# One GpSimd shift for two pattern groups, and two changes to the zero products, in a two-attention kernel

## The chip, the core and the metric

The kernel runs on one core of one Trainium2 chip. The metric is the device time of one launch in microseconds (us), and a smaller time is better. A core has a matrix engine (TensorE; PE in the profile, with its weight loads listed apart as PEld), a vector engine (VectorE, DVE), a scalar engine (ScalarE, ACT), GpSimd (POOL), and an engine that here only issues transfers (SyncE, SP). Each works through its own list of instructions in order and waits at semaphores for the others.

## The reference, cut to what matters

Two independent attention blocks A and B work on inputs of 2048 rows by 512 columns in bfloat16, with 32 heads of width 16; their outputs are joined side by side.

```python
# A: linear attention
phi = lambda t: jnp.where(t > 0, t + 1, jnp.exp(t)) + 1e-6
pq, pk = phi(q), phi(k)
kv  = jnp.einsum("bhsd,bhse->bhde", pk, v)
num = jnp.einsum("bhqd,bhde->bhqe", pq, kv)
den = jnp.einsum("bhqd,bhd->bhq", pq, jnp.einsum("bhsd->bhd", pk))[..., None] + 1e-6
a = merge_heads(num / den) @ wo
# B: softmax attention
scores = jnp.einsum("bhqd,bhkd->bhqk", q, k) * 16 ** -0.5
p = softmax(scores)
b = merge_heads(jnp.einsum("bhqk,bhkd->bhqd", p, v)) @ wo
out = jnp.concatenate([a, b], axis=-1)
```

B's scores are 32 heads of 2048 by 2048 numbers, each of which needs an exponential. That is nearly all of the work.

## The kernel before, in words

**Units and blocks.** B is cut into 32 units: four groups of eight heads, times four pieces of 512 queries, times two halves of the eight heads (`unit`). In a unit, four heads stand in four row strips of TensorE (`g` = 0 to 3), and the 2048 keys are cut into 16 pieces of 128, so a unit has 64 blocks of 128 keys by 512 queries. For each block `qk` (L807) makes the scores in PSUM, something takes the exponential, and a product with the values (L1142) adds the block to the unit's sum in `PVb` (pPV in the profile). A column of ones beside the values gives the softmax denominator.

**Two ways to an exponential.** Most blocks go the ACT way: two or three blocks lie side by side in one of two PSUM slots of `S5` (pS), and one ScalarE instruction (L1018) writes their exponentials to `PT`. The others go the D way: their scores go to a bank of `DB` (pD) or to a spare bank of pS, and VectorE (L923) turns them into 16-bit integers whose bits, read as float16, are a rough exponential. `DI` holds eight groups of up to two such blocks. To refine the result, two more patterns are made by adding a constant to the integers of the whole group (`shift`, for v = 1 and v = 2). GpSimd does this (L1071), or for v = 2 now and then VectorE (L1068). A block of the D way thus takes three products L1142 instead of one: with the values `VV` for the first two patterns and with scaled values `VX` for one.

**The rest.** In between lie "jobs": projections of q, k and v for later units, all of attention A (with exponentials `EA`, L630, on ScalarE), its output projections (L745) and some checks of the input's size. At a unit's end VectorE transposes pPV (L1171), takes reciprocals, and GpSimd normalizes (L1177).

**Who sets the order.** Nothing is chosen on the chip. While the kernel is built, a planner keeps an estimated clock `T` for each engine, holds candidates (`push`, `cands`, `pv_cand`, `job_cand`, `fill_act_cand`, `fill_d_cand`), and picks again and again the one that could start first. A priority breaks ties. It then writes the instruction into that engine's list. Estimated durations stand at each `push`, and the constants at the head of the function bound the choices: `PW` weighs groups not yet shifted in GpSimd's backlog, `JM` is the number of PSUM banks that jobs may hold, `DBL` and `PBL` bound the backlogs of VectorE and GpSimd at which blocks still take the D way, `FPB` and `FDB` bound when a third block may go to ScalarE, `PTA` tells when `PT` is scarce, `PSH` and `DSH` decide which engine shifts v = 2, and `PM` is when GpSimd's result counts as ready, measured from its estimated end. So a change of a constant or of one choice moves everything that follows.

**Zero products.** TensorE is kept busy in places by products with a tile of zeros: `warm` (L1255) issues 30 at the very start, and `fill_in` (L1399) puts some in when the planner sees TensorE waiting for its next step.

**Start and end.** The first two tiles of x come by a transposing load, the next two are transposed by TensorE (L1266), and then the first projections (L1277) lead to the first scores. After the last unit, VectorE works through its two halves (L1232 to L1237), and the last output projections of B (L1194) and four stores (L1247) follow.

Of the kernel before, what the change touches and what calls it, by code (L numbers as in the profile page):

```python
# [9 lines left out]
F16 = mybir.dt.float16  # L10
I16 = mybir.dt.int16
ACTF = mybir.ActivationFunctionType
ALU = mybir.AluOpType
# [225 lines left out]
def bass_concat_heads__linear_attn_block__softmax_full_mha__prompt_kernel(nc, A_x, A_wqkv, A_wo, B_x, B_wqkv, B_wo, out):  # L239
# [6 lines left out]
    NU = NGP * NC * 2  # L246
    SC = 0.25
    VST = 136
    LAY = (25, 8)
    PW = 0.7  # L250
    JM = 2
    JX = 1
    NB = 2
    NPT = LAY[0]
# [11 lines left out]
    ALAG = 100.0  # L266
    DLEAD = 0.8
    DPR = 3.0
    DBL = 2.0
    PBL = 7.0  # L270
    SEG = ()
    GB = 0.0
    PM = -0.05
    AEND = 60.0
    RW = 0.3
    EQ = 26.0
    FPB = 5.0
    FDB = 1.5
    FNR = 2
    AJP = 2.5  # L280
    HP = 0.5
# [1 line left out]
    BJ0 = 30.0  # L283
    D0 = 14.0
    RMX = 4
    XAL = 7.0
    NZ = 0
    SD = 0
    PTA = 4
    PTD = 1  # L290
    PSH = 2.5
    DSH = 1.0
    FM = 0.06
    JB = True
    WARM = (30,)
    TRACE = None


# [5 lines left out]
    with es:  # L304
# [629 lines left out]
                waiting[bi] = (buf, b, push("dve", en + LAT, 0, 0.6, p1))  # L934

        dgroup["st"] = {}

        def bank_at(at):

# [114 lines left out]
        def chain(buf):  # L1054
            s_ = dgroup["st"][buf]
            if not s_["closed"] or len(s_["items"]) < s_["taken"]:
                return
            s_["chained"] = True
            n = len(s_["items"])
            w = 512 * n  # L1060
            src = DI[:, buf, D0_:D0_ + w]
            rk = [("DI", 0, buf, i) for i in range(n)]

            def shift(v, t_):
                def r(st_, en_, lane="pool"):
                    if lane == "dve":
                        wide = w + 32
                        sch.add(lane, lambda e: e.tensor_scalar(gapped(DI[:, buf, :], DIV[v], wide // 32, 32), DI[:, buf, D0_ - 32:D0_ + w], 1.0, float(SHIFT[v - 1]),  # L1068
                                                                op0=ALU.mult, op1=ALU.add), reads=rk, writes=[("DI", v, buf)])
                    else:  # L1070
                        sch.add(lane, lambda e: e.tensor_scalar(DI[:, buf, DIV[v]:DIV[v] + w], src, 1.0, float(SHIFT[v - 1]), op0=ALU.mult, op1=ALU.add),  # L1071
                                reads=rk, writes=[("DI", v, buf)])
                    for i, b in enumerate(s_["items"]):
                        if lane == "dve":
                            P = gapped(DI.bitcast(F16)[:, buf, :], DIV[v] + 33 + i * 528, 16, 32)
                        else:
                            P = DI.bitcast(F16)[:, buf, DIV[v] + i * 512:DIV[v] + (i + 1) * 512]
                        pv_ready[b[0]].append((en_ + (PM if lane == "pool" else LPE["dve"]), b, (P, ("DI", v, buf)), ("d", buf), "VX"[v - 1]))
                if v == 2 and p_backlog(t_) - DSH * d_backlog(t_) > PSH:
                    push("dve", t_, 1, 0.06 + (w + 32) * 0.00053, lambda st_, en_: r(st_, en_, "dve"))  # L1080
                else:
                    push("pool", t_ + LAT + 0.05, 0, 0.276 + w * 0.00083, r)
            for v in (1, 2):
                shift(v, s_["t"])

# [80 lines left out]
        def unit_done(u, t_):  # L1166
# [96 lines left out]
        for t, bk, lane in ((2, SBANKS[1], "dve"), (3, SBANKS[2], "act")):  # L1263
            def tr(e, t=t, bk=bk):
                for cc in range(4):
                    ins = e.transpose(bfv(bk)[:, cc * 128:(cc + 1) * 128], ONL[:, t, cc * 128:(cc + 1) * 128], identb[:])  # L1266
# [143 lines left out]
        while True:  # L1410
# [157 lines left out]
```

## Time and profile before

| | |
|---|---|
| time of three runs | 673.05, 674.85, 674.97 us; median 674.85 |
| the profiled execution | 674.9 us, of which its span, first to last instruction, is 673.2 us |
| instructions in the span | 16020 |
| data read from and written to HBM | 4.46 MB and 4.19 MB |

The profile names a group of instructions by engine, by line of the kernel and by what it writes and reads (`out<-in`). In the table of groups, "x" is the number of instructions, then come the group's busy time in us and the mean duration of one in ns, and after the bar the engine's idle time just before them with what ended it. Instructions of one engine overlap: the next one begins while the one before it is still finishing. A mean duration is thus longer than the distance from one to the next. The chain of waits follows the last instruction backwards through whatever released each step, and its pieces do not overlap.

### The profile page before, as it was taken

To read this page: it belongs to the slowest core of one execution; us is meant where nothing else is said; L and a number is where in the kernel's file an instruction comes from. 1 tells how busy PE (TensorE), PEld (TensorE's weight loads), DVE (VectorE), ACT (ScalarE), POOL (GpSimd) and SP (SyncE) were. 2 spreads that over 40 slices of the span, in tenths; PEclk is the share of its full clock that TensorE was granted. 3 is DMA by queue.
4 is the path that set the end of the run, shared out by engine and by line. 5 is a ranking of instruction groups with operands and counts; after the bars stand their busy time and mean duration, and the time that the engine had idled before them with its cause. 6 is when DMAs were issued, how large, how long until landed. Compare 5 with 4: busy or idle time off the path is not lost.

```text
span 673.2 us, 16020 instructions
## 1 busy us (share of the span) xinstructions
PE 651.9 (97%) x6628; PEld 204.4 (30%) x6628; DVE 623.5 (93%) x1051; ACT 657.4 (98%) x691; POOL 589.7 (88%) x603
## 2 busy tenths in 40 slices
PE   8999999999999999999999999999999999999997
PEld 5323332223333333222222322322224222222222
DVE  3999999999989999999999999999999999999993
ACT  5999999999999999999999999999999999999995
POOL 5898898998989998989898999989899889898893
PEclk9999999999999999999999999999999999999999
DMA  9602001101011101110111110100000010001101
GB/s 215 161 2 33 1 9 34 40 10 38 4 33 32 32 2 33 34 47 10 40 40 18 32 25 25 17 9 10 9 25 2 17 33 33 1 33 41 32 33 37
DMA packets 53216, 21.56 MB, mean 32 GB/s; under 512 B 44176, under 2 KB 52624, under 8 KB 53136
## 3 DMA queue, kind: packets, MB, share of 16 engines
q1 hardware_dynamic: 51808, 19.94, 12.7%
q8 instruction: 54, 0.88, 0.5%
q10 hardware_dynamic: 1328, 0.52, 0.3%
q14 instruction: 26, 0.21, 0.1%
HBM read 4.46 MB, written 4.19 MB: 13 GB/s over the span
## 4 chain that ended last, share of the span: by engine, by line
ACT 93%; PE 5%; DVE 1%; DMA 1%; issue 0%; ACTq 0%
ACT PT L1018 90%; ACT EA L630 2%; PE pPV L1142 1%; PE pS L807 1%; DVE DI L923 1%; PE pD L745 1%; DMA xTb<-in_B_x_dram 1%; PE pS L1277 0%; PE pS L1399 0%; PE pS L1194 0%; DVE KNa L519 0%; PE pD L1277 0%; DVE OT L1171 0%; PE pD L1194 0%; ACTq L1512 0%
## 5 line engine op out<-in xcount | busy, mean ns | idle before, releaser
L1018 ACT ACTIVATE PT<-pS 128x1024 f16<-128x1024 f32 (+1 forms) x652 | 648.5, 1307 | 2.7 <-PE pS L807 2.3
L1071 POOL TENSOR_SCALAR DI<-DI 128x1024 int16<-128x1024 int16 x529 | 553.1, 1046 | 60.7 <-DVE DI L923 24.2
L923 DVE TENSOR_SCALAR DI<-pD 128x512 int16<-128x512 f32 (+1 forms) x453 | 315.0, 710 | 20.3 <-PE pD L807 12.4
L807 PE MATMUL pS<-QT,KM 32*128 32x512 bf16 x1570 | 256.8, 385 | 12.1 <-ACT PT L1018 7.7
L1142 PE MATMUL pPV<-PT,VV 128*17 128x512 f16 x1397 | 238.3, 381 | 0.3 <-ACT PT L1018 0.3
L1142 PE MATMUL pPV<-DI,VV 128*17 128x512 f16 x1302 | 216.7, 381 | 0.6 <-DVE OT L1171 0.4
L807 PE MATMUL pD<-QT,KM 32*128 32x512 bf16 x478 | 166.6, 384 | 0.2
L1142 PE MATMUL pPV<-DI,VX 128*17 128x512 f16 x651 | 156.1, 384 | 0.0
L807 PEld LDWEIGHTS pS<-QT,KM 32*128 32x128 bf16 x1570 | 65.0, 91 | 264.6 <-ACT PT L1018 224.4
L923 DVE TENSOR_SCALAR DI<-pS 128x512 int16<-128x512 f32 x173 | 117.2, 678 | 1.6 <-PE pS L807 1.1
L1068 DVE TENSOR_SCALAR DI<-DI 128x1056 int16<-128x1056 int16 x123 | 83.9, 686 | 0.7
L1142 PEld LDWEIGHTS pPV<-PT,VV 128*17 128x17 bf16 x1397 | 49.2, 88 | 44.5 <-issue 37.3
L1142 PEld LDWEIGHTS pPV<-DI,VV 128*17 128x17 bf16 x1302 | 44.9, 88 | 41.7 <-issue 33.5
L807 PEld LDWEIGHTS pD<-QT,KM 32*128 32x128 bf16 x478 | 39.5, 91 | 9.0 <-DVE DI L923 2.8
L1142 PEld LDWEIGHTS pPV<-DI,VX 128*17 128x17 bf16 x651 | 34.3, 88 | 20.1 <-issue 16.7
L655 PE MATMUL pD<-Wa,xTa 128*128 128x256 bf16 x232 | 35.1, 275 | 0.5 <-DVE DI L923 0.2
L537 PE MATMUL pD<-xTb,Wb 128*128 128x512 bf16 x84 | 24.9, 384 | 0.2
L630 ACT ACTIVATE EA<-pD 128x512 bf16<-128x512 f32 x28 | 23.0, 821 | 0.0
L655 PEld LDWEIGHTS pD<-Wa,xTa 128*128 128x128 bf16 x232 | 18.1, 97 | 15.6 <-DVE DI L923 6.9
L1171 DVE STREAM_TRANSPOSE OT<-pPV 128x512 f32<-128x512 f32 x31 | 21.8, 704 | 0.0
L1177 POOL TENSOR_TENSOR OT<-OT,ZR 128x256 bf16<-128x256 f32 x31 | 19.3, 622 | 2.6 <-DVE ZR L1176 1.6
L621 POOL TENSOR_SCALAR VX<-VV 128x544 bf16<-128x544 bf16 x16 | 10.3, 646 | 8.2 <-DVE VV L618 7.1
(142 smaller groups left out, 359.1 us busy)
## 6 DMA issues: line engine op xcount, KB each, us to landing
out_dram<-KNa SPq DMA_DIRECT2D x32, 128.0 KB, 1.7
Wa<-in_A_wqkv_dram SPq DMA_DIRECT2D x1, 1536.0 KB, 8.1
KM<-KR SPq DMA_DIRECT2D x96, 16.0 KB, 1.8
Wb<-in_B_wqkv_dram SPq DMA_DIRECT2D x2, 384.0 KB, 5.4
Wb<-in_B_wqkv_dram SPq DMA_DIRECT2D x1, 512.0 KB, 4.3
Wa<-in_A_wo_dram SPq DMA_DIRECT2D x1, 512.0 KB, 4.0
Wa<-in_B_wo_dram SPq DMA_DIRECT2D x1, 512.0 KB, 3.8
ON<-in_B_x_dram ACTq DMA_DIRECT2D x1, 256.0 KB, 2.7
```

The source lines that it names most:

```text
L537: return e.matmul(f32v(bk), lhsT=Wb[:, cc, kind * 512 + Gp * 128:kind * 512 + Gp * 128 + 128], rhs=xTb[:, cc, sc * 512:(sc + 1) * 512], st ...
L621: st.append(("pool", 0.7, f_op("pool", lambda e: e.tensor_scalar(VX[:, r, 4 * t4:4 * t4 + 4, :].rearrange("p t c -> p (t c)"), VV[:, r, 4 ...
L630: ("act", 0.052 + n * 0.000833, f_ev("act", lambda e, bk: e.activation(EA[:, 0:n], f32v(bk)[:, c0:c0 + n], ACTF.Exp), [], ["EA"])),
L655: return e.matmul(f32v(bk)[:, 256 * tt:256 * tt + 256], lhsT=xTa[:, b, cc, (o + tt) * 128:(o + tt + 1) * 128], rhs=Wa[:, cc, 512 * kind + ...
L807: return e.matmul(dst, lhsT=KM[32 * g:32 * g + 32, Gp % 2, e_, j * 128:(j + 1) * 128], rhs=QT[32 * g:32 * g + 32, Gp % 2, c * 512:(c + 1) ...
L923: sch.add("dve", lambda e: e.tensor_scalar(DI[:, buf, D0_ + i * 512:D0_ + (i + n) * 512], f32v(DBANK[b0], n * 512), ESC, EB, op0=ALU.mult, ...
L1018: sch.add("act", lambda e: e.activation(PTf[:, p0 * 512:p0 * 512 + w], S5[:, c0:c0 + w], ACTF.Exp, scale=SC), reads=skeys(sl, len(bl)), wr ...
L1068: sch.add(lane, lambda e: e.tensor_scalar(gapped(DI[:, buf, :], DIV[v], wide // 32, 32), DI[:, buf, D0_ - 32:D0_ + w], 1.0, float(SHIFT[v ...
L1071: sch.add(lane, lambda e: e.tensor_scalar(DI[:, buf, DIV[v]:DIV[v] + w], src, 1.0, float(SHIFT[v - 1]), op0=ALU.mult, op1=ALU.add), reads= ...
L1142: sch.add("pe", lambda e, g=g, j=j, c0=c0, V_=V_, r2=r2, P=P, first=first, last_=last_: e.matmul(PVb[32 * g:32 * g + 17, 0:512] if len(P.s ...
L1171: sch.add("dve", lambda e: e.transpose(OT[:, 0, :], PVb[:, 0:512]), reads=[("PV", g) for g in range(4)], writes=[("OT", 0)])
L1177: ("pool", 0.8, f_op("pool", lambda e: e.tensor_tensor(xn[:, :, 16 * e_:16 * e_ + 16], o[:, :, 0:16], zr.unsqueeze(2).broadcast_to([128, 1 ...
```

## The change

Four things are edited.

1. When GpSimd starts a shift and the same shift of another group of the same width is ready as well (`PMW` = 0), both are written as one instruction over two of the groups in `DI`. The planner reckons it at 0.276 us plus 0.83 ns for each of its 2048 elements per partition.
2. `fill_in` subtracts 0.8 us instead of `FM` = 0.06 us from the wait that it fills, once all units are done.
3. `warm` is called a second time, with 8 products, between the two transposes at the start and the first projections.
4. Constants of the planner change, and its estimate for the normalization on GpSimd goes from 0.8 to 0.7 us.

Line numbers in this text are those of the kernel before. In the changed kernel the same lines lie 2 to 23 lines lower (L807 becomes L809, the shift L1071 becomes L1094).

```diff
-    PW = 0.7
-    JM = 2
+    PW = 0.4
+    JM = 1
...
-    DBL = 2.0
+    DBL = 2.5
...
-    PM = -0.05
+    PM = -0.1
...
-    FPB = 5.0
-    FDB = 1.5
+    FPB = 4.0
+    FDB = 2.0
...
+    PMW = 0.0
+    SLK = {}
...
-    PTA = 4
+    PTA = 6
...
-    DSH = 1.0
+    DSH = 0.5
...
-    WARM = (30,)
+    WARM = (30, 8)
...
+        pshift = []
...
+            def give(buf_, v, lane, en_):
+                for i, b in enumerate(dgroup["st"][buf_]["items"]):
...
             def shift(v, t_):
...
+                def on_pool(st_, en_):
+                    two = [x for x in pshift if x[0] == v and x[2] == w and x[1] != buf and x[3][0] <= st_ + PMW]
+                    pshift.remove(me[0])
+                    bufs, keys = [buf], rk
+                    if two:
+                        o = min(two, key=lambda x: x[3][2])
+                        pshift.remove(o)
+                        cands["pool"].remove(o[3])
+                        bufs, keys = sorted((buf, o[1])), rk + o[4]
+                        st_ = max(st_, o[3][0])
+                        T["pool"] = en_ = st_ + 0.276 + 2 * w * 0.00083
+                    sl = slice(bufs[0], bufs[-1] + 1, max(bufs[-1] - bufs[0], 1))
+                    sch.add("pool", lambda e: e.tensor_scalar(DI[:, sl, DIV[v]:DIV[v] + w], DI[:, sl, D0_:D0_ + w], 1.0, float(SHIFT[v - 1]), op0=ALU.mult, op1=ALU.add),
+                            reads=keys, writes=[("DI", v, x) for x in bufs])
+                    for x in bufs:
+                        give(x, v, "pool", en_)
                 if v == 2 and p_backlog(t_) - DSH * d_backlog(t_) > PSH:
-                    push("dve", t_, 1, 0.06 + (w + 32) * 0.00053, lambda st_, en_: r(st_, en_, "dve"))
+                    push("dve", t_, 1, 0.06 + (w + 32) * 0.00053, on_dve)
                 else:
-                    push("pool", t_ + LAT + 0.05, 0, 0.276 + w * 0.00083, r)
+                    me = [(v, buf, w, push("pool", t_ + LAT + 0.05, 0, 0.276 + w * 0.00083, on_pool), rk)]
+                    pshift.append(me[0])
...
-                  ("pool", 0.8, f_op("pool", lambda e: e.tensor_tensor(xn[:, :, 16 * e_:16 * e_ + 16], o[:, :, 0:16],
+                  ("pool", 0.7, f_op("pool", lambda e: e.tensor_tensor(xn[:, :, 16 * e_:16 * e_ + 16], o[:, :, 0:16],
...
+        warm(WARM[1])
...
-            n = min(int((st - T["pe"] - FM) / 0.107), 24)
             u = pvu[0]
+            n = min(int((st - T["pe"] - (FM if u < NU else 0.8)) / 0.107), 24)
...
+            dur = dur * SLK.get(eng, 1.0)
```

More of the change, by code (lines that the diff above doesn't have):

```diff
@@ L1062, in chain @@
             rk = [("DI", 0, buf, i) for i in range(n)]
-            def shift(v, t_):
[L1065 to L1078, printed above, removed]
@@ new lines, in give @@
+            def give(buf_, v, lane, en_):
+                for i, b in enumerate(dgroup["st"][buf_]["items"]):
+                    if lane == "dve":
+                        P = gapped(DI.bitcast(F16)[:, buf_, :], DIV[v] + 33 + i * 528, 16, 32)
+                    else:
+                        P = DI.bitcast(F16)[:, buf_, DIV[v] + i * 512:DIV[v] + (i + 1) * 512]
+                    pv_ready[b[0]].append((en_ + (PM if lane == "pool" else LPE["dve"]), b, (P, ("DI", v, buf_)), ("d", buf_), "VX"[v - 1]))
@@ new lines, in shift, with on_dve @@
+            def shift(v, t_):
+                def on_dve(st_, en_):
+                    wide = w + 32
+                    sch.add("dve", lambda e: e.tensor_scalar(gapped(DI[:, buf, :], DIV[v], wide // 32, 32), DI[:, buf, D0_ - 32:D0_ + w], 1.0, float(SHIFT[v - 1]),
+                                                             op0=ALU.mult, op1=ALU.add), reads=rk, writes=[("DI", v, buf)])
+                    give(buf, v, "dve", en_)
+                def on_pool(st_, en_):
[14 more added lines that the diff above has]
+                        give(x, v, "pool", en_)
```

## The prediction

> **What bounds the kernel now.** I read the page first: the engines' busy time and the chain of waits. Then came the groups by form and the list of waits, to see whether the bounding engine ever stood still, and last its own stretch in the windows and the chain in pieces.
>
> ```profile
> PE 651.9 (97%) x6628; PEld 204.4 (30%) x6628; DVE 623.5 (93%) x1051; ACT 657.4 (98%) x691; POOL 589.7 (88%) x603
> ACT 93%; PE 5%; DVE 1%; DMA 1%; issue 0%; ACTq 0%
> ...
> L1018 ACT ACTIVATE PT<-pS 128x1024 f16<-128x1024 f32 x557 | 550.4, 1247 | 0.4 <-issue 0.4
> L1018 ACT ACTIVATE PT<-pS 128x1536 f16<-128x1536 f32 x94 | 156.9, 1669 | 2.3 <-PE pS L807 2.3
> ...
> PEld pS L807 <- ACT PT L1018: 224.4, 521, 0.9
> ...
> 10.29:663.98 653.69, 653.28 (x684) 1.00 0.12 29
> ...
> 181.79 0.49 ACT EA L630
> 182.28 7.33 ACT PT L1018 x8
> 366.22 6.84 ACT PT L1018 x7
> ```
>
> Four engines look nearly full, so shares alone decide nothing. The chain does: 93% of it is ScalarE. From its first exponential at 10.29 us to its last end at 663.98 us ScalarE is busy 653.28 of 653.69 us, and the groups show one idle stretch of 0.4 us after the first wait of 2.3 us. TensorE meanwhile waits 521 times for ScalarE to give a score slot back. So the time is a start of 10.29 us, ScalarE's work, and an end of 673.2 - 663.98 = 9.2 us.
>
> The chain gives ScalarE's real prices, since its pieces do not overlap. Eight exponentials of 1024 take 7.33 us, or 0.916 each. Seven take 6.84 us; six of them at 0.916 leave 6.84 - 5.50 = 1.34 for one of 1536. A 512 takes 0.49. Before, 94 x 1.343 + 557 x 0.916 + 33 x 0.489 (32 for attention A, one last score block) = 652.6 us, 1.1 below the stretch. ScalarE has practically no holes to fill, and only less work for it, an earlier start or a shorter end can help.
>
> **Less work on ScalarE.** The order of the changed kernel, written out per engine, has 571 exponentials of 1024 (14 more), 82 of 1536 (12 fewer) and the same 33 of 512. That is 14 x 0.916 - 12 x 1.343 = 12.8 - 16.1 = **-3.3 us**: eight of 2048 blocks leave ScalarE for the D way. This holds if those who now do more stay hidden.
>
> ```profile
> L923 DVE TENSOR_SCALAR DI<-pD 128x512 int16<-128x512 f32 x428 | 284.6, 680 | 19.1 <-PE pD L807 11.4 <-PE pS L807 5.4
> L923 DVE TENSOR_SCALAR DI<-pD 128x1024 int16<-128x1024 f32 x25 | 30.4, 1216 | 1.2 <-PE pD L807 1.0
> L1068 DVE TENSOR_SCALAR DI<-DI 128x1056 int16<-128x1056 int16 x123 | 83.9, 686 | 0.7
> L1071 POOL TENSOR_SCALAR DI<-DI 128x1024 int16<-128x1024 int16 x527 | 551.9, 1047 | 60.5 <-DVE DI L923 24.2
> L1071 POOL TENSOR_SCALAR DI<-DI 128x512 int16<-128x512 int16 x2 | 1.2, 621 | 0.1
> ...
> 308.22 10.03 POOL L1071 TENSOR_SCALAR DI<-DI 128x1024 int16<-128x1024 int16 x9 [0.22 <-DVE DI L923]
> ...
> PEld pPV L1142 <- POOL DI L1071: 1.6, 7, 0.2
> ```
>
> VectorE evicts six fewer single blocks (601 to 595), seven more pairs (25 to 32), and does four whole shifts fewer and one half shift more: at most -6 x 0.68 + 7 x 1.22 - 4 x 0.69 + 0.4 = +2.1 us. L923 alone stands idle 20 us for scores, so it fits.
>
> GpSimd: the order has 425 single shifts, 57 joined ones, and one of half width. In a full run nine singles take 10.03 us, so one follows the next at (10.03 - 1.05) / 8 = 1.12. No trace here has a joined shift. Its lower price comes from the slope between 512 and 1024 elements, (1.047 - 0.621) / 512 = 0.83 ns each: 1.12 + 1024 x 0.83 ns = 1.97 us. Its upper price is two singles, 2.25, if a second group costs a whole instruction's overhead again. I take 1.97, since the contents of each group lie as before. Then shifting costs 425 x 1.12 + 57 x 1.97 = 588 us against 527 x 1.12 = 590 before, although 23 more block shifts run on GpSimd; at 2.25 it would be 604. Both fit into the 60 us that L1071 stood idle.
>
> What a joined shift does cost is latency: the first group's pattern is there 0.85 us later than alone, its `DI` group comes free that much later, and TensorE's products with it wait in a list that also holds ScalarE's next scores. The planner reckons with this in the order. The cover is ScalarE's queue: an exponential of 1024 lasts 1.247 us on average but they follow at 0.916, so the next one's scores stand ready on average 0.33 us before they are needed. TensorE now waits only 1.6 us in all for GpSimd. `PM`, moved by 0.05 us, lengthens such waits by at most 0.05. TensorE itself gets 16 more products L1142. I put **+0.4 us** for new holes, with bounds of 0 and 4 (57 joins at 0.07). The other constants work only through the counts above, the job banks included.
>
> [...]
>
> **Eight more products at the start.** These rows are from the chain and the timeline, with the groups of 256-column products below them.
>
> ```profile
> 0.81 5.07 DMA xTb<-in_B_x_dram
> ...
> 6.01 2.42 PE L1277 MATMUL pS<-xTb,Wb 128*128 128x128 bf16 x12 [0.71 <-DMA xTb<-in_B_x_dram]
> 6.53 1.41 PEld L1277 LDWEIGHTS pS<-xTb,Wb 128*128 128x128 bf16 x8 [0.20 <-DMA Wb<-in_B_wqkv_dram]
> 8.22 1.49 PE L1277 MATMUL pD<-xTb,Wb 128*128 128x128 bf16 x8
> 9.64 0.82 PE L807 MATMUL pS<-QT,KM 32*128 32x512 bf16 x5
> 10.60 1.04 PE L537 MATMUL pD<-xTb,Wb 128*128 128x512 bf16 x4
> ...
> 1.06 3.38 PE L1255 MATMUL pD<-ZW 128*128 128x128 bf16 x30 [1.06 <-DVE ZR L428]
> 4.23 1.06 PE L1266 MATMUL pS<-identb,ON 128*128 128x128 bf16 x8
> ...
> L1277 PE MATMUL pS<-xTb,Wb 128*128 128x256 bf16 x8 | 1.9, 415 | 0.0
> L1399 PE MATMUL pPV<-xTb,ZW 128*17 128x256 bf16 x11 | 2.0, 275 | 0.0
> ```
>
> The clock row of the page shows 9 throughout, but the durations say otherwise: the first projections take 415 ns for 256 columns, later products of that width 275. Thirty products of 128 columns start within 4.23 - 1.06 = 3.17 us, 0.106 each; at 10.6 us products of 512 columns follow at (1.04 - 0.38) / 3 = 0.22, a single one taking 0.38. So TensorE runs at half rate until about 10 us and at full rate after that. It works without a break from 1.06 to about 5.3, waits 0.71 us for x, and is at full rate some 4 to 4.6 us after it resumes at 6.01.
>
> The eight products take 8 x 0.106 = 0.85 us. They follow the transposes at about 5.08 and end about 5.93, so the wait for x covers them; uncovered they would cost 0.85. They close the break, so the run-up counts from 1.06 and full rate should come by 6 to 7 us. The query projections still wait for weights until 6.53. From there 16 products take until about 9.5 at half rate, 3 us, and half as long at full rate: -1.5. The first scores gain about 0.2 more (0.65 us from their start to the exponential, of which a third goes by 275 against 415), while VectorE's evictions between them give 0.1 back. **-1.6 us**, with ends at -1.75 (full rate from the first projection) and +0.1 (no change of rate). ScalarE's two lists agree in their first 29 exponentials, so nothing new stands in the way there, and the gain reaches the whole train.
>
> [...]
>
> **The end.** From the timeline of TensorE, VectorE and SyncE:
>
> ```profile
> 664.40 0.38 PE L1142 MATMUL pPV<-PT,VV 128*17 128x512 f16 x1
> 664.72 1.04 PE L1194 MATMUL pS<-Wa,ON 128*128 128x512 bf16 x4
> 665.68 1.15 PE L1399 MATMUL pS<-Wb,ZW 128*17 128x256 bf16 x9
> 666.77 0.60 PE L1194 MATMUL pD<-Wa,xTb 128*128 128x512 bf16 x2
> 667.30 1.37 PE L1399 MATMUL pS<-Wb,ZW 128*17 128x256 bf16 x11
> 668.60 0.60 PE L1194 MATMUL pS<-Wa,xTb 128*128 128x512 bf16 x2
> ...
> 666.68 0.20 DVE L1233 RECIPROCAL ZR<-OT 128x8 f32<-128x8 f32 x1
> 667.24 0.45 DVE L1237 STREAM_TRANSPOSE xTb<-OT 128x256 bf16<-128x256 bf16 x1
> 669.25 0.69 DVE L519 CAST KNa<-pS 128x512 bf16<-128x512 f32 x1 [1.56 <-PE pS L1194]
> ...
> 667.82 3.48 SPq L1247 DMA_DIRECT2D out_dram<-KNa  x4
> ...
> KNa<-VNa SPq DMA_TRANSPOSE x16, 2.4
> ```
>
> Twenty zero products stand among the last projections. VectorE is done at 667.69, yet the last pair starts at 668.60, behind eleven zeros. Their removal alone gives 668.60 - 667.75 = -0.85 us. But the new order puts other work there: after the last product L1142 come six L1194, then the last projection of A (four L745), then six more L1194 that were done earlier before. These 16 follow at 0.22 each, 3.5 us, so the first of the final four starts about 3.8 us after the last L1142. Worse, VectorE copies A's projection between its two halves: from about 2.7 us (0.32 + 10 x 0.22 + 0.16 to the result) to 3.3, then L1233 to L1237 of the second half (1.01 us) until 4.35. The last products go at 4.4 and 4.6, against 4.2 and 4.4 before, and SyncE has A's store ahead of the four. I take **+0.3 us**, between -0.85 and +1.5 (the upper end if A's late transposing load, 2.4 us from issue to landing ahead of L745, holds TensorE).
>
> **Sum.** 674.9 - 3.3 - 1.6 + 0.3 + 0.4 = **670.7 us**, from the profiled execution (span 673.2 and 1.7 around it), whose 674.9 is also the median of the three runs, 674.85. About 0.3% of the time, 2 us, is what a measurement can tell from no change, so 672.8 is the border to faster.
>
> **Rivals.** (1) *The rate does not change early*, because a short break remains (the weights at 6.53) or zeros count for less. Against it, breaks of 0.2 us did not stop the rise after 6.01. The time would be 674.9 - 3.3 + 0.1 + 0.3 + 0.4 = 672.4. (2) *ScalarE gets holes of a few us*, since fewer triple exponentials and late patterns make the order tighter: at the bound of 4 us, 674.3, the same as before. For it speaks that VectorE and GpSimd are both over 88% busy; against it, one hole in 651 exponentials. (3) *Slower: TensorE stands at products with joined patterns.* If each of the 57 joins held it 0.33 us beyond the mean lead, plus the 0.05 of `PM`, often enough to starve ScalarE by 0.15 us, that would be 8.6 us, giving 674.9 - 3.3 - 1.6 + 0.3 + 8.6 = 678.9. It decides from about 0.12 us per join (6.8 us in all). The seven short waits for GpSimd speak against it. (4) *The end costs its upper price*: 671.9, still faster. That the joins are not made is excluded by the order.
>
> **How the numbers follow.** The forecast with its own bounds, 669.0 to 672.5, including (4), gets 0.62. Rival (1) gets 0.14, most of it just below the border; (2) 0.14, and (3) 0.10. Faster: 0.62 + 0.10 = 0.72; same: 0.04 + 0.13 = 0.17; slower: 0.10 + 0.01 = 0.11. The range is 669.0 (all lower ends: 674.9 - 3.3 - 1.75 - 0.85) to 674.3 (rival 2), which leaves out the slower case and the tails.
>
> **What would show it.** Right: the first L1018 at about 8.7 instead of 10.29 and first projections at 275 ns; 57 shifts of 2 x 1024 near 1.9 us long; ScalarE's stretch at 650 to 651 us with no idle row above 1 us; no L1399 after the last L1142, but L745 there, and 9.2 to 10 us from the last exponential to the end. Wrong: idle ScalarE behind scores, with the wait of L1142 for L1071 grown far above 1.6 us; joined shifts above 2.25; or an end over 10.7 us.

## The result, and the profile after

The changed kernel takes 676.52 us (median of 20 runs, 674.26 to 678.62), the kernel before on the same chip 674.50 (20 runs, 672.91 to 675.91). The ratio is 1.0039 with a 95% interval of 1.0028 to 1.005: slower by 0.4%, where 670.7 us and faster had been forecast. The profiled execution took 678.33 us, with a span of 676.6.

First the page of the changed kernel (engines and chain), the groups of ScalarE and GpSimd by form, one row of the waits, and ScalarE's busy time from its first exponential to the last one's end:

```profile
PE 650.5 (96%) x6632; PEld 202.6 (30%) x6632; DVE 626.5 (93%) x1049; ACT 654.7 (97%) x693; POOL 589.1 (87%) x557
ACT 92%; PE 3%; DMA 1%; DVE 1%; SPq 1%; issue 0%; ACTq 0%
...
L1021 ACT ACTIVATE PT<-pS 128x1024 f16<-128x1024 f32 x571 | 557.8, 1242 | 3.5 <-PE pD L809 2.0 <-PE pS L809 1.5
L1021 ACT ACTIVATE PT<-pS 128x1536 f16<-128x1536 f32 x82 | 136.5, 1665 | 2.2 <-PE pS L809 1.7 <-PE pD L809 0.5
...
L1094 POOL TENSOR_SCALAR DI<-DI 128x1024 int16<-128x1024 int16 x425 | 443.9, 1044 | 52.6 <-DVE DI L925 23.7
L1094 POOL TENSOR_SCALAR DI<-DI 128x2048 int16<-128x2048 int16 x57 | 108.2, 1897 | 8.8 <-DVE DI L925 5.7
...
PEld pPV L1162 <- POOL DI L1094: 2.4, 11, 0.2
...
8.64:663.95 655.31, 650.62 (x686) 0.99 0.13 29
```

The counts are those of the order (571, 82, 57 joined shifts), and a joined shift takes 1.897 us. TensorE's products still hardly wait for patterns: 2.4 us in eleven waits, none over 0.2. But ScalarE now stands idle for 655.31 - 650.62 = 4.7 us of its stretch, where it was 0.4, and the stretch has grown from 653.69 to 655.31 although its work shrank. Behind the last exponential the span runs on for 676.6 - 663.95 = 12.65 us, where it was 9.2. Only the start did as forecast: the first exponential comes at 8.64 instead of 10.29.

So the profiled 678.33 comes out as 674.9 - 3.3 (work) - 1.65 (start) + 4.9 (ScalarE late) + 3.4 (end) = 678.3. The 4.9 is the growth of the stretch, 1.6, plus the 3.3 of work that went. Three places hold nearly all of the last two terms.

**Near 530 us.** ScalarE, VectorE, GpSimd and TensorE from the timelines, then TensorE's granted clock (after the engines' busy times) in two windows, and last the masked product of the kernel before:

```profile
523.99 6.75 ACT L1021 ACTIVATE PT<-pS 128x1024 f16<-128x1024 f32 x7
531.42 1.45 ACT L1021 ACTIVATE PT<-pS 128x1536 f16<-128x1536 f32 x1 [0.69 <-PE pS L809]
533.38 1.02 ACT L1021 ACTIVATE PT<-pS 128x1024 f16<-128x1024 f32 x1 [0.51 <-PE pD L809]
535.20 1.94 ACT L1021 ACTIVATE PT<-pS 128x1024 f16<-128x1024 f32 x2 [0.79 <-PE pS L809]
537.55 1.02 ACT L1021 ACTIVATE PT<-pS 128x1024 f16<-128x1024 f32 x1 [0.41 <-PE pD L809]
539.07 2.37 ACT L1021 ACTIVATE PT<-pS 128x1536 f16<-128x1536 f32 x2 [0.49 <-PE pD L809]
...
527.96 0.68 DVE L925 TENSOR_SCALAR DI<-pD 128x512 int16<-128x512 f32 x1
528.56 1.77 DVE L589 TENSOR_TENSOR GRW<-GRW,ZMk 128x32 f32<-128x32 f32 x1
530.25 0.68 DVE L925 TENSOR_SCALAR DI<-pS 128x512 int16<-128x512 f32 x1
...
528.39 1.90 POOL L1094 TENSOR_SCALAR DI<-DI 128x2048 int16<-128x2048 int16 x1
...
530.99 0.39 PE L809 MATMUL pS<-QT,KM 32*128 32x512 bf16 x3 [1.08 <-DVE DI L925]
531.59 0.38 PE L809 MATMUL pD<-QT,KM 32*128 32x512 bf16 x1 [0.21 <-DVE GRW L587]
532.17 0.64 PE L1162 MATMUL pPV<-DI,VV 128*17 128x512 f16 x2
...
530.00:535.00 5.00, 3.81 (x35) 0.92 (x35) 4.61 (x10) 3.21 (x3) 3.42 (x4) 0.71 0.00 0
535.00:540.00 5.00, 5.00 (x52) 1.16 (x52) 3.69 (x7) 3.89 (x4) 3.65 (x4) 0.61 0.02 3
...
L587 DVE TENSOR_TENSOR GRW<-GRW,ZMk x2: 183/400/618, 522.1 to 530.8; 128x32 f32<-128x32 f32 x2
```

The chain can be read upwards from ScalarE. Its idle rows end with scores, which TensorE gives late. TensorE stood 1.08 us for VectorE's eviction L925, and from 532 us on a product takes 0.64 instead of 0.38 us, at a granted clock of 0.71 and 0.61. VectorE was late because L589, a product of 32 elements per partition that masks a result of the size check, took 1.77 us. GpSimd's joined shift ran from 528.39 to 530.29 us; L589 ended at 530.33. Before (as L587) its two instances took 618 and 183 ns, and the longer one ended 33 ns after a single shift.

**Near 598 us.** ScalarE and TensorE again, and the reads of the size flag by TensorE's weight loads and by ScalarE:

```profile
597.80 2.37 ACT L1021 ACTIVATE PT<-pS 128x1024 f16<-128x1024 f32 x2 [1.07 <-PE pD L809]
...
596.74 0.39 PE L809 MATMUL pS<-QT,KM 32*128 32x512 bf16 x2 [0.85 <-ACT PT L1021]
...
L1534 PEldq TENSOR_LOAD <-FLG x1: 626/626/626, 595.9 to 595.9; - x1
L1534 ACTq TENSOR_LOAD <-FLG x1: 461/461/461, 597.2 to 597.2; - x1
```

In this stretch every engine reads the size flag (`FLG`) into a register, 0.46 to 0.63 us each, which the timeline does not count as busy. TensorE reads before ScalarE, from 595.85 us on, and gives the next scores only at 596.74. ScalarE, whose exponential before ended at 596.73, gets them at 597.13, and its own read follows from 597.16 to 597.62: the two reads add up to a hole of 1.07 us. In the kernel before the same reads left a hole of 0.4 us at 567 us.

**The end.** TensorE, SyncE's issues (one row spans all four, the next is the second of them), and the DMA view from 671.9 us on, then from 671.95 on for the last store alone (the last number is the median from issue to landing):

```profile
664.38 1.47 PE L1214 MATMUL pS<-Wa,ON 128*128 128x512 bf16 x6
665.69 1.03 PE L747 MATMUL pD<-Wa,KNa 128*128 128x512 bf16 x4
...
668.06 0.95 PE L1214 MATMUL pS<-Wa,xTb 128*128 128x512 bf16 x3
...
668.88 3.54 SPq L1267 DMA_DIRECT2D out_dram<-KNa  x4
669.37 2.08 SPq L1267 DMA_DIRECT2D out_dram<-KNa  x1
...
q8 instruction: 1, 0.02, 2.0%
...
out_dram<-KNa SPq DMA_DIRECT2D x2, 128.0 KB, 2.8
...
out_dram<-KNa SPq DMA_DIRECT2D x1, 128.0 KB, 3.8
```

TensorE is on time. Its last product starts near 668.06 + 2 x 0.22 = 668.5, 4.55 us after the last exponential; before, it was 668.60 + 0.22 - 663.98 = 4.84. What is late comes behind it: the second of SyncE's four issues takes 2.08 us where the others take 0.33 to 0.45, and the last store, issued at 671.98, lands at 675.77, 3.8 us later. Both lie beside loads of 16 KB of instructions (queue q8), one from 669.4 to 670.7 and one from 673.1 to 674.6 us.

### The profile page after: what moved, and what is told of

Same layout as the page of the kernel before. It is cut to its first block, busy times and chain, and to the rows that moved or that the text cites. A ratio compares the mean times of both kernels' runs of the same rounds, so it can differ in the third digit from the quotient of the medians.

```text
span 676.6 us, 15985 instructions
## 1 busy us (share of the span) xinstructions
PE 650.5 (96%) x6632; PEld 202.6 (30%) x6632; DVE 626.5 (93%) x1049; ACT 654.7 (97%) x693; POOL 589.1 (87%) x557
## 4 chain that ended last, share of the span: by engine, by line
ACT 92%; PE 3%; DMA 1%; DVE 1%; SPq 1%; issue 0%; ACTq 0%
ACT PT L1021 90%; ACT EA L632 2%; PE pPV L1162 1%; DMA xTb<-in_B_x_dram 1%; PE pS L809 1%; SPq L391 1%; DVE DI L925 1%; PE pS L1214 0%; DVE GRW L589 0%; PE pD L747 0%; PE pD L584 0%; PE pD L1214 0%; ACT KNa L521 0%; PE pD L705 0%; DVE GRW L587 0%
## 5 line engine op out<-in xcount | busy, mean ns | idle before, releaser
L1094 POOL TENSOR_SCALAR DI<-DI 128x1024 int16<-128x1024 int16 (+1 forms) x483 | 552.6, 1144 | 61.5 <-DVE DI L925 29.4
L925 DVE TENSOR_SCALAR DI<-pD 128x512 int16<-128x512 f32 (+1 forms) x450 | 316.6, 717 | 21.2 <-PE pD L809 16.2
L809 PE MATMUL pS<-QT,KM 32*128 32x512 bf16 x1566 | 258.1, 386 | 12.7 <-ACT PT L1021 5.2
L1162 PE MATMUL pPV<-PT,VV 128*17 128x512 f16 x1389 | 235.5, 384 | 0.3 <-ACT PT L1021 0.2
L1162 PE MATMUL pPV<-DI,VV 128*17 128x512 f16 x1318 | 220.7, 384 | 0.7 <-DVE OT L1191 0.7
L809 PE MATMUL pD<-QT,KM 32*128 32x512 bf16 x482 | 163.3, 386 | 0.2 <-DVE GRW L587 0.2
L1162 PE MATMUL pPV<-DI,VX 128*17 128x512 f16 x659 | 158.5, 385 | 0.0
L809 PEld LDWEIGHTS pS<-QT,KM 32*128 32x128 bf16 x1566 | 65.2, 91 | 267.4 <-ACT PT L1021 222.1
L925 DVE TENSOR_SCALAR DI<-pS 128x512 int16<-128x512 f32 x177 | 119.9, 677 | 2.5 <-PE pS L809 1.7
L1078 DVE TENSOR_SCALAR DI<-DI 128x1056 int16<-128x1056 int16 x120 | 81.4, 684 | 0.4
L1162 PEld LDWEIGHTS pPV<-PT,VV 128*17 128x17 bf16 x1389 | 48.5, 88 | 46.3 <-issue 39.5
L1162 PEld LDWEIGHTS pPV<-DI,VV 128*17 128x17 bf16 x1318 | 45.3, 88 | 41.6 <-issue 33.2
L809 PEld LDWEIGHTS pD<-QT,KM 32*128 32x128 bf16 x482 | 38.7, 91 | 8.1 <-DVE DI L925 2.5
L1162 PEld LDWEIGHTS pPV<-DI,VX 128*17 128x17 bf16 x659 | 33.7, 88 | 19.6 <-issue 15.6
L657 PE MATMUL pD<-Wa,xTa 128*128 128x256 bf16 x216 | 32.6, 275 | 0.5 <-DVE DI L925 0.4
L539 PE MATMUL pD<-xTb,Wb 128*128 128x512 bf16 x92 | 27.5, 384 | 1.7 <-DMA xTb<-in_B_x_dram 1.0
L657 PEld LDWEIGHTS pD<-Wa,xTa 128*128 128x128 bf16 x216 | 16.9, 98 | 14.2 <-issue 6.3
L521 DVE CAST KNa<-pD 128x512 bf16<-128x512 f32 x22 | 15.0, 683 | 4.6 <-PE pD L747 4.6
```

The lines of the kernel that those rows point to most:

```text
L521: return lambda e, bk: (e.tensor_copy(out_fn(), in_fn(bk)) if lane == "dve" else e.activation(out_fn(), in_fn(bk), ACTF.Copy))
L539: return e.matmul(f32v(bk), lhsT=Wb[:, cc, kind * 512 + Gp * 128:kind * 512 + Gp * 128 + 128], rhs=xTb[:, cc, sc * 512:(sc + 1) * 512], st ...
L657: return e.matmul(f32v(bk)[:, 256 * tt:256 * tt + 256], lhsT=xTa[:, b, cc, (o + tt) * 128:(o + tt + 1) * 128], rhs=Wa[:, cc, 512 * kind + ...
L809: return e.matmul(dst, lhsT=KM[32 * g:32 * g + 32, Gp % 2, e_, j * 128:(j + 1) * 128], rhs=QT[32 * g:32 * g + 32, Gp % 2, c * 512:(c + 1) ...
L925: sch.add("dve", lambda e: e.tensor_scalar(DI[:, buf, D0_ + i * 512:D0_ + (i + n) * 512], f32v(DBANK[b0], n * 512), ESC, EB, op0=ALU.mult, ...
L1078: sch.add("dve", lambda e: e.tensor_scalar(gapped(DI[:, buf, :], DIV[v], wide // 32, 32), DI[:, buf, D0_ - 32:D0_ + w], 1.0, float(SHIFT[v ...
```

## The experiments

All times are medians in us; ratios are to the kernel before on the same chip. Line numbers are the changed kernel's.

**The start alone.** To the kernel before, only the eight products are added; and, apart from that, only the end's zero products are cut.

```diff
+        warm(8)                                                     # b_warm8
```
```diff
-            n = min(int((st - T["pe"] - FM) / 0.107), 24)           # b_nozero
+            n = min(int((st - T["pe"] - (FM if u < NU else 0.8)) / 0.107), 24)
```

> The kernel before with one edit: eight more zero products ahead of the first projections. The first exponential should start at about 8.65 us instead of 10.29 in either theory. Theory 1 (the forecast): the whole gain stays, so the time is about 1.6 us below the kernel before. Theory 2 (the gain meets a load): with TensorE ahead, its 16 KB instruction load falls at about 12 us, into the transposing load of x's third quarter, which then lands near 15.1 instead of 12.65; ScalarE stands idle about 0.8 us near 16 us, and only about 0.8 us is left.

> The kernel before with one edit: 0.8 us are subtracted from the waits filled with zero products after the last unit, which leaves 6 of the 20 zeros at the last projections. Forecast: the last pair of projections no longer stands behind zeros, and the time falls by 0.8 to 0.85 us. [...]

b_warm8: 673.59 (673.31 to 674.13, 12 runs), ratio 0.9994, interval 0.9986 to 1.0003. b_nozero: 672.97 (672.26 to 674.54), ratio 0.9989, 0.9979 to 0.9999. The first exponentials of each, b_warm8 first, from ScalarE's timeline:

```profile
8.77 2.36 ACT L1018 ACTIVATE PT<-pS 128x1536 f16<-128x1536 f32 x2 [1.05 <-PE pS L807]
```
```profile
8.88 2.37 ACT L1018 ACTIVATE PT<-pS 128x1536 f16<-128x1536 f32 x2 [1.05 <-PE pS L807]
```

b_nozero missed its own forecast of 0.8 to 0.85 us less: its median is 0.6 lower, and the end of its profiled execution is 8.8 us long instead of 9.2, so fewer zeros are worth about 0.4 there.

b_warm8 starts as early as forecast, and yet its median is no better. The second row tells why: b_nozero has no extra products at the start, but this execution of it was early all the same, with its first exponential at 8.88 us. The kernel before has two sorts of executions. Its 35 runs on the chip of b_warm8 are 19 between 672.9 and 673.9 and 16 between 674.6 and 675.2; b_warm8 has one group. That the groups are early and late starts fits the three traces without the extra products: the late one (10.29) is of 674.9 us, the early ones (b_nozero, and b_hook below with 8.67) of 673.1 and 673.3. So the eight products only turn the late part of the executions into early ones, which lowers the mean by 0.4 us (674.0 to 673.6). The execution from which -1.6 was worked out was a late one; against it b_warm8's profiled 673.5 is 1.4 lower.

Part of the early start is lost again at x's third quarter. The transposing load of the changed kernel, and of the kernel before, issued at 6.7 us, and the one packet of instructions in the changed kernel's window 11.9 to 12.1:

```profile
xTb<-in_B_x_dram SPq DMA_TRANSPOSE x1, 8.4
...
q8 instruction: 1, 0.02, 68.9%
```
```profile
xTb<-in_B_x_dram SPq DMA_TRANSPOSE x1, 6.0
```

The instruction load starts at 12.0 us and ends at 14.2; packets of x stand until 15.0, and ScalarE idles 0.7 us at 16.2. In the kernel before that load starts at 14.4, when x's quarter has landed. b_warm8 has the same hole at 15.9 us, with 0.3. The early start alone does not make it: b_nozero and b_hook start as early, their load comes at 13.9 and 13.1, and they have no hole there. That the instruction load causes it was not tested.

**The masked product and the joined shift.** a_nomask leaves the masked product out (a step of the size check, whose limit is raised with it), in the same order otherwise; a_split keeps the order, but writes each joined shift as two single ones.

```diff
-                        ("dve", 0.15, f_op("dve", lambda e: e.tensor_tensor(gw, gw, ZMk[:]...          # a_nomask
+                        ("dve", 0.15, lambda bk: None),
```
```diff
-                    sch.add("pool", lambda e: e.tensor_scalar(DI[:, sl, ...], DI[:, sl, ...], ...     # a_split
+                    for x in bufs:
+                        sch.add("pool", lambda e, x=x: e.tensor_scalar(DI[:, x, ...], DI[:, x, ...], ...
```

> The changed kernel without the product of the head sums with the mask (VectorE, two operands in SBUF, 128x32, twice in the program) that is part of the check of the input's size; its threshold is raised so that the same branch is taken. Planner and order are otherwise the same. Theory A: this product waited 1.8 us for GpSimd's joined shift, TensorE then stood still for 1.1 us, and its clock fell to half for 6.8 us in some runs. Then no run shows half clock near 530 us, the holes of ScalarE near 531 to 539 (3.4 us in the profiled run) are gone, and the times have one group at 674 to 676.5 instead of two, median about 675. Rival B: the order there is too tight whatever VectorE does; then the holes and the two groups stay, median about 676.5.

> The changed kernel with each of the 57 joined shifts written as two single ones in the same place of GpSimd's list, waiting for the same inputs; order of all else unchanged. If joining itself hurts by its length (results and buffers late, VectorE locked out), the time falls below that of the changed kernel by 1 us or more; the masked product then waits at most 1.05 us instead of 1.77. If joining helps as planned, GpSimd needs 0.25 us more at 57 places, TensorE waits more for it than before, and the time rises by up to a few us over 676.5.

a_nomask: 674.63 (673.87 to 675.16, 12 runs), 1.0011, 1.0002 to 1.0019. a_split: 675.34 (673.22 to 675.99), 1.0008, 0.9996 to 1.0021. a_nomask in the two windows of above, and a_split's masked product:

```profile
530.00:535.00 5.00, 4.74 (x72) 1.46 (x64) 4.87 (x11) 5.00 (x7) 4.68 (x5) 1.00 0.02 3
535.00:540.00 5.00, 4.71 (x56) 1.42 (x49) 4.84 (x8) 5.00 (x6) 4.61 (x5) 1.00 0.00 0
```
```profile
L589 DVE TENSOR_TENSOR GRW<-GRW,ZMk x2: 784/876/969, 529.5 to 532.7; 128x32 f32<-128x32 f32 x2
```

Without the product the clock stays at 1.00, ScalarE is busy throughout, and the runs form one group; the changed kernel's 20 runs are ten at a mean clock of 0.997 or more (median 675.9) and ten at 0.994 or less (678.2), of which the profiled one is one. With single shifts the product takes 0.8 to 1.0 us instead of 1.8, and no run's mean clock is under 0.996. The median is 1.2 us below the changed kernel's, as expected if joining hurts by its length. Its times still lie in two groups (four from 673.2 to 673.6, eight from 675.0 to 676.0), which the clock does not explain; why was not found. So the length of the joined shift matters, through a product on VectorE that has nothing to do with patterns.

**How the product waits.** a_mask8 writes it as eight instructions of four columns, each with one tensor in SBUF and a mask value per partition; a_mask8_hook has the late flag reads (below) besides. a_mp moves the product to GpSimd.

```diff
-("dve", 0.15, f_op("dve", lambda e: e.tensor_tensor(gw, gw, ZMk[:]...                               # a_mask8
+("dve", 0.15, f_op("dve", lambda e: [e.tensor_scalar(gw[:, :, h], gw[:, :, h], ZMk[:, h:h + 1], None, op0=ALU.mult) for h in range(8)][-1],
```
```diff
-("dve", 0.15, f_op("dve", lambda e: e.tensor_tensor(gw, gw, ZMk[:]...                               # a_mp
+("pool", 0.3, f_op("pool", lambda e: e.tensor_tensor(gw, gw, ZMk[:]...
```

> The changed kernel with the masked product L589 written as eight instructions over 4 columns each, with one tensor operand and a mask value per partition, in the same place; all other lists are the same. Theory (the instruction with two operands in SBUF waits until GpSimd's joined shift is done, 1771 ns): eight short ones take 0.4 to 0.8 us together although GpSimd is shifting, no half clock, one group of runs, median 674.6 to 674.9 as without the product. Rival (any further step at that place makes TensorE late): half clock in about half of the runs, median 676 or more.

> The same with TensorE's, ScalarE's and VectorE's reads of the size flag at the end: the complete kernel with both repairs. Theory: as a_sum, 671.7 to 672.2, ScalarE idle under 1 us in all, faster than the kernel before by 1.5 to 2 us. Rival: the eight instructions cost ScalarE a hole of over 0.5 us near 530 us, 672.5 or more.

> The changed kernel, but the masked product L589 runs on GpSimd instead of VectorE. The planner's order changes with it: 575 exponentials of 1024, 80 of 1536, 33 of 512 on ScalarE (1.0 us more work than the changed kernel by 0.916, 1.343 and 0.489), 48 joined shifts, and A's last projection comes ahead of the last units instead of behind them. Theory (half clock in about half of the runs comes from that product waiting behind a joined shift; the long end comes from A's fifth store behind the last exponential): no half clock anywhere, one group of runs, end 9 to 9.5 us, median 672 to 673. Rival (the end doesn't depend on A's store): end over 12 us, median 675 to 676.

a_mask8 was a miss: 680.63 (680.01 to 681.39, 4 runs), 1.0104, 1.0088 to 1.0119; a_mask8_hook 677.43 (676.84 to 678.93), 1.0055, 1.0042 to 1.0069. The product in a_mask8, from the view by tile and from VectorE's timeline:

```profile
L589 DVE TENSOR_SCALAR GRW<-GRW,ZMk x16: 217/220/1749, 528.3 to 535.4; 128x4 f32<-128x4 f32 x16
...
528.28 2.67 DVE L589 TENSOR_SCALAR GRW<-GRW,ZMk 128x4 f32<-128x4 f32 x8
```

The first one of the eight still takes 1749 ns and ends 26 ns after GpSimd's joined shift (528.11 to 530.01). Two more meet a single shift and end 25 and 26 ns after it (477 and 1085 ns long). So the theory of its expectation, that the two operands in SBUF make VectorE wait, falls. (The mask values lie in SBUF too, so it stays open whether the second source or the form of the instruction makes it wait.) In the changed kernel the shift L1078 (16-bit, a constant as second operand) has a mean of 684 ns and never takes over 703 beside GpSimd, and the evictions L925 of 512 columns from PSUM have a mean of 679 and never take over 693.

The ends of these waits agree: 25, 26 and 26 ns after a shift in a_mask8, 37 and 38 in the changed kernel (the 479 and 1771 ns of L589), and 33 in the kernel before. What VectorE and GpSimd share there, no run shows.

The eight also cost 2.67 instead of 1.77 us, and the time rises by 4 us over the changed kernel. Part of that is the half clock: all ten runs of the two kernels have a mean clock of 0.994 or less, and over the changed kernel's own such runs (678.2) a_mask8 loses 2.4. Near 530 us VectorE has no slack at all (busy 5.80 of 5.80 us from 527.4 to 533.2 us in the changed kernel), and the masked product was the worst place to lose a microsecond.

a_mp came as forecast: 672.91 (672.49 to 674.18, 12 runs, all at a clock of 0.998 or more), 0.9983, 0.9973 to 0.9992. Its order differs (575 exponentials of 1024, 80 of 1536, 48 joins), and A's last projection lies ahead of the end there: the end is 9.7 us long. Its third store issue takes 1.79 us beside an instruction load, so a slow issue alone does not make the long end; its last store lands 1.8 us after its issue, not 3.8.

**The end, and the flag.** a_hold makes TensorE, ScalarE and VectorE wait for the last landing before the branch that ends the program; a_actq lets ScalarE issue three of the last four stores; a_latehook moves the three engines' flag reads to the end of their lists.

```diff
+            if queue in ("pe", "act", "dve"):                                                          # a_hold
+                e.wait_ge(sems[stores[-1].lane], 16 * stores[-1].count)
             with e.If(got[0] > THRESHOLD_BITS):
```
```diff
-                                              reads=kst(tl), queue="sp", force_signal=True))          # a_actq
+                                              reads=kst(tl), queue="sp" if tl == 3 else "act", force_signal=True))
```
```diff
-            sch.emit_queue(queue, e, sems, hook=(flag_op.idx + 200, hook))                             # a_latehook
+            sch.emit_queue(queue, e, sems, hook=(10 ** 9 if queue in ("pe", "act", "dve") else flag_op.idx + 200, hook))
```

> The changed kernel, but TensorE, ScalarE and VectorE wait for the landing of the last store before they take the branch that ends the program. Theory (their branch starts a 16 KB instruction load, which stalls SyncE's second store issue for 2.1 us and holds up the last store's packets): no 16 KB load between the last exponential and the last landing, that issue takes 0.3 to 0.5 us, the last store lands 1.8 to 2.0 us after its issue; the span ends 9.5 to 11 us after the last exponential (12.6 in the changed kernel), the loads that now follow the landing included; median 674 to 675. Rival (SyncE stalls because five stores stand in its queue): the issue still takes 1.9 us or more and the end is 12.5 to 14 us, median 676.5 to 678.

> The changed kernel, but three of the last four stores are issued by ScalarE, which made their copies, instead of by SyncE. Theory A (the end is long because SyncE issues five stores one behind the other and stalls in one): last store issued 6.3 to 6.7 us after the last exponential instead of 8.0, end 10 to 11 us, median 674.5 to 675.5. Theory B (the end is long because the last store's packets stand behind a 16 KB instruction load): the store is issued earlier, but lands when it did, end 12 us or more, median 676 to 677.

> The changed kernel, but TensorE, ScalarE and VectorE read the size flag at the end of their lists instead of in the middle of the last units. Theory (each engine's read of about 0.5 us opens the ScalarE hole of 1.2 us near 594 to 598 us, because TensorE and ScalarE read one after the other there): that hole goes, the end gets no longer because the reads lie beside the last stores; median 1.0 to 1.2 us under the changed kernel's, 675.4. Rival (the hole comes from late scores, the read only lies in it): hole of 0.7 us or more stays in that place, median within 0.4 us of the changed kernel's 676.5.

a_hold: 676.88 (675.39 to 678.89), 1.0035, 1.0021 to 1.0049. SyncE's four issues, the last two stores, and then the DMA view from 672.2 us on:

```profile
668.79 1.87 SPq L1267 DMA_DIRECT2D out_dram<-KNa  x4
...
out_dram<-KNa SPq DMA_DIRECT2D x2, 128.0 KB, 1.8
...
q8 instruction: 1, 0.02, 1.9%
```

The mechanism is as expected: with no 16 KB instruction load beside them the four issues take 1.87 instead of 3.54 us, the last two stores land 1.8 us after their issue instead of 2.8 in the median, and the last one is there 8.2 us after the last exponential instead of 11.8. The time is no better, and both the median and the end of 12.2 us miss what was expected, 674 to 675 and 9.5 to 11: branch and instruction load now follow the landing, and the span ends 676.0 - 672.05 = 4 us after it. So what the issues and the landing no longer pay is paid behind the landing here.

a_actq: 676.29 (675.48 to 678.43), 1.0039, 1.0025 to 1.0053, as long as the changed kernel. So SyncE's serial issues alone are not the cause. In its profile the last store was issued at 670.25 and landed at 672.13, with an end of 10.9 us, so theory B's late landing did not show either; the median says that this execution, the fastest of its nine, is not the rule.

a_latehook: 673.65 (672.96 to 676.79), 1.0003, 0.9988 to 1.0017, 2.9 under the changed kernel where 1.1 was expected. Six of its eleven runs keep the clock at 0.997 or more; compared among such runs (673.3 against 675.9), or among those with the half clock (675.5 against 678.2), it is 2.6 to 2.7 less. The profiled execution is one with the half clock. ScalarE's timeline has no hole near 598 us:

```profile
589.72 11.23 ACT L1021 ACTIVATE PT<-pS 128x1024 f16<-128x1024 f32 x11
```

The rest came from the end, 10.9 instead of 12.65 us: the reads delay the branches, the instruction load starts 6.5 us after the last exponential instead of 5.5, and SyncE's issues are nearly through by then (2.93 us for the four).

**Both repairs, and both on the kernel before.** a_sum is a_nomask with the late reads; a_mp_hook, b_hook and b_all are a_mp, the kernel before, and the kernel before with the eight products and without zeros at the end, each with the late reads.

> The changed kernel without the masked product L589 (that step of the size check is left out, and the limit of the check raised) and with TensorE's, ScalarE's and VectorE's reads of the size flag at the end. Theory (half clock after the masked product, the flag's hole and the late store are separate losses): the two edits add up; each alone gave 674.6, and 673.3 to 673.7 in runs without half clock against 675.9 of the changed kernel's own such runs, so 674.6 - 2.5 = 672.1 median, one group of runs, end of 10.5 to 11.2 us, ScalarE idle under 0.6 us. Rival (they hide one another): 673.3 or more.

> The changed kernel with the masked product on GpSimd and the three reads of the size flag at the end. Theory: the hole of 0.42 + 0.14 us near 598 to 601 us goes, end 9.2 to 9.7 us, median 672.2 to 672.4 against 672.9 without the late reads. Rival: the reads cost at the end what they save in the middle, 672.9.

> The kernel before with the three reads of the size flag at the end. Theory: ScalarE's hole of 0.5 us at 567 goes, and the 16 KB instruction load at the end comes later, so that SyncE's store issue of 1170 ns shortens to 450 to 800: median 0.6 to 1.0 under the kernel before. Rival: no hole matters that is 0.5 us wide, same time.

> The kernel before (its planner's constants, no joined shifts) with the eight warm products, without zero products at the end and with the late reads of the size flag. Theory: 673.0 (without end zeros) - 0.5 to 0.8 (flag) - 0.3 (start no longer in two groups) = 672.0, no slower than the changed kernel with the same repairs, since 2.3 us less ScalarE work there is eaten by its holes and its longer end. Rival (the joined shifts keep their gain): the changed kernel with its repairs is faster than this one by 1 us or more.

a_sum: 671.69 (671.32 to 672.58, 8 runs), 0.9971, 0.9961 to 0.9981; the two losses add up. Its ScalarE groups and stretch:

```profile
L1020 ACT ACTIVATE PT<-pS 128x1024 f16<-128x1024 f32 x571 | 558.5, 1248 | 0.5 <-PE pS L808 0.5
L1020 ACT ACTIVATE PT<-pS 128x1536 f16<-128x1536 f32 x82 | 137.7, 1679 | 1.0 <-PE pS L808 1.0
...
8.80:659.31 650.51, 649.99 (x686) 1.00 0.13 30
```

With one idle row of 0.5 us inside the stretch (the 1.0 is the wait for the first exponential), it is 650.5 us long, as forecast for the changed kernel, with all 57 joins in it.

b_hook was a miss: 674.39 (672.77 to 674.83), 1.0004, 0.9994 to 1.0013. Its hole is gone, but the last issue still took 1.36 us, and the runs lie in two groups, so 0.5 us could hide in them. b_all missed its 672.0: 673.45 (672.82 to 674.14), 0.9993, 0.9984 to 1.0002. a_mp_hook: 672.69 (672.50 to 673.18, 11 runs), 0.9982, 0.9973 to 0.9991, no more than 0.2 below a_mp: its hole at the flag reads is gone, but its end is 10.4 us long where 9.2 to 9.7 was expected, so most of the gain is paid there, as its rival said. It is the fastest complete version, 0.2% ahead of the kernel before and 0.6% (3.8 us of medians) ahead of the changed one. Against b_all it keeps 0.8 us of its 2.3 us less ScalarE work: less than the 1 us of the rival, more than the nothing of the theory. a_sum, which leaves a step out, is 1.8 below b_all.

## Why the prediction was wrong

**Less work on ScalarE, -3.3: right.** It shows where the holes are repaired: a_sum's stretch is 650.51 against 653.69, 3.2 less.

**The start, -1.6: right for one execution, wrong as a price.** Clock, products and first exponential came as worked out: the first projections (L1298) take at most 288 ns where those of 256 columns took 415, and the exponential comes at 8.64 us. But -1.6 was taken from a late execution and added to a median of executions that are early half of the time. By the medians of b_warm8 it is nothing that can be measured, by the means 0.4. That the break of 0.71 us holds the rise back, as the term assumes, was the author's estimate and no run shows it: b_nozero stood for 1.57 us between 3 and 8 us and was early all the same. Rival (1) did not happen.

**New holes, +0.4: the step that failed first.** It measured 4.9. By the idle rows, three places make up 4.3 of it: 0.7 at x's third quarter, 1.1 at the flag reads, and 2.9 near 530 us, less the 0.4 that was there before. The other 0.6 is ScalarE's busy time, which fell by 2.7 instead of 3.3 us: an exponential that stands alone between holes takes 1.02 us where one in a train adds 0.916. Some 2.3 us of the loss come and go with the half clock (678.2 against 675.9). The cover that was named, ScalarE's lead of 0.33 us, was real and did hide the late patterns: L1162 waited 2.4 us in all. What was not asked is who else stands still while GpSimd runs 1.9 us. GpSimd's own mean of 1047 ns cannot show it, since the one who waits is VectorE. The row to look for was there: L587 of the kernel before, 32 elements per partition in 183 and in 618 ns.

**The end, +0.3, between -0.85 and +1.5: the other step that failed.** It measured +3.4. The list of products and copies was worked out well, and TensorE was even earlier by 0.3. The price lay in stores and instruction loads, of which the sum had only the word that SyncE has A's store ahead of the four. Counted from the last exponential, the last store was issued 1.1 us later than before (8.0 against 6.9), landed 2.0 us later after its issue (3.8 against 1.8), and 0.3 us more followed the landing. In the kernel before, SyncE's timeline had a sign of it, an issue that took over three times as long as its neighbours:

```profile
669.65 1.17 SPq L1247 DMA_DIRECT2D out_dram<-KNa  x1
```

Rival (4) had the right direction and under half of the size.

**Rival (3)** had the sign and the culprit, the joined shift, but by another road: not TensorE waiting for patterns in 57 places, but VectorE held in one.

**What stays open:** why the clock falls in only half of the runs, whether the hole at x's third quarter is the instruction load's, how much of the end each of the two 16 KB loads costs, and why a_split has two groups. How long TensorE stands does not decide alone about the clock: in b_nozero it stood for 1.57 us between 3 and 8 us, longer than the 1.29 near 530 us, and the first exponential came at 8.88 us all the same, near the 8.77 of b_warm8.

## What to carry to other kernels

Before an instruction of one engine is made longer, list what the other engines do that cannot run beside it, however small, and price the longest wait at the place where that engine has no slack. Price a gain at the start over several executions, not one, and price an end up to the landing of the last store, with the instruction loads that the closing branch sets off.

## What the runs showed of the hardware

- A VectorE operation on SBUF of 4 or 32 elements per partition took up to 1771 ns (32 elements in the changed kernel; 1749 for 4 in a_mask8), ending 25 to 38 ns after the GpSimd instruction beside it. Evictions from PSUM of 512 columns (mean 679 ns, at most 693) and the 16-bit shift by a constant (mean 684, at most 703) did not wait.
- In the changed kernel TensorE's clock fell to 0.50 for 6.8 us, from 532.1 to 538.9 us, after TensorE had stood for 1.08 and 0.21 us between 529.9 and 531.6 us. Without the masked product (a_nomask) it stayed at 1.00 there.
- In the changed kernel one issue took 2.08 us beside a 16 KB instruction load, where the others took 0.33 to 0.45, and a store landed 3.8 us after its issue beside another, where the kernel before took 1.8. In a_hold no such load lay beside the four issues and the last two landings: the issues took 1.87 us together, the landings came 1.8 us after their issue, and the program ended 4 us after the last one.
